# Channel attention on one core: TensorE waits for VectorE's partial sums, which are joined every third tile

## The chip, the cores and the metric

The kernel runs on 1 core of one Trainium2 chip. The metric is the device time of one execution in microseconds (us). Time before: median 527.9 us.

## The reference, cut to what matters

```python
# x: (1, 384, 384, 384) bfloat16, w1d: (1,) bfloat16
g = jnp.einsum("bhwc->bc", x) / (H * W)          # mean of every channel
s = jax.nn.sigmoid(g * w1d[0])                   # one factor for each of 384 channels
return x * s[:, None, None, :]
```

The input is 113.25 MB and so is the output. The factor depends on the mean over all of x, so taken literally x would be read twice. The kernel reads it once: it guesses the factors from the first 4 rows of the first tile, multiplies all tiles by the guess while it sums them, and at the end compares the true factors with the guess after rounding to bfloat16. Only if they differ does a second pass run. With the given inputs it doesn't.

## The kernel before

x is cut into 18 tiles of 64 rows a partition (6.29 MB). Four buffers hold them in turn. For each tile SyncE issues the load, TensorE adds up 48 rows with matmuls against a matrix of ones, VectorE adds up the other 16 rows and then multiplies the whole tile in place by the guess (the gate), and ScalarE's queue issues the store. The load of tile k + 4 waits until the store of tile k has landed.

```python
TILE, SLOTS, EARLY, LEAD, FORE, OWN = 64, 4, 4, 8, 32, 16
PAUSE = 9
...
def one(e, s):                                   # TensorE, one tile
    e.wait_ge(ready, 1).then_inc(ready, -1)      # the tile has landed
    for r, n in ((0, FORE), (FORE, TILE - OWN - FORE)):
        add_rows(e, 1, (slot(s) + r) * C, n, False, False).then_inc(plan.sems["tensor"], 1)
...
def sum_own(k):                                  # VectorE: 16 rows to one, then into the running sum
    plan.op("vector", lambda e: e.reduce_sum(to[:], view, axis=mybir.AxisListType.X), ...)
    if k:
        plan.op("vector", lambda e: e.tensor_tensor(own[:], own[:], part[:], ALU.add), ...)
...
def pause(r0):                                   # ScalarE: delays the fifth load
    to = at(base, PAUSE)
    plan.op("scalar", lambda e: e.activation(
        to, warm[:, 0:1].broadcast_to([P, PAUSE * C]), ACT_F.Sigmoid), ...)
```

At the end VectorE splits its running sum into three bfloat16 terms, TensorE adds these over the partitions, VectorE adds TensorE's three banks with six instructions (`add_banks`), ScalarE makes the true factors, and VectorE compares them and writes a flag. SyncE, ScalarE and VectorE read the flag to decide on the second pass.

## Time and profile before

| | before |
|---|---|
| median of the first 3 runs | 527.9 us (527.87 to 527.96) |
| span of the profiled run | 526.5 us |
| VectorE busy | 440.0 us, 78 instructions |
| DMA | 226.5 MB, 430 GB/s over the span |
| flag written | 521.4 us |
| last store issued, landed | 502.9, 526.4 us |

The busy shares, the DMA row and the chain of waits are shown in the prediction. Here is one steady tile on VectorE from the timeline of the kernel before (start, duration, engine, line, operation; in brackets the idle time and who ended it): the sum of 16 rows, the add, the gate.

```profile
170.19 10.56 DVE L338 TENSOR_REDUCE part<-arena 128x384 f32<-128x6144 bf16 x1 [4.94 <-DMA arena<-in_x_dram]
180.78 0.56 DVE L345 TENSOR_TENSOR own<-own,part 128x384 f32<-128x384 f32 x1
181.26 12.95 DVE L210 TENSOR_TENSOR arena<-arena,s_early 128x24576 bf16<-128x24576 bf16 x1
```

VectorE works 24 of 29 us and waits 4.94 us for the load. It has room, and the load is what it waits for.

### The profile page before, as it was taken

To read this page: it belongs to the slowest core of one execution; us is meant where nothing else is said; L and a number is where in the kernel's file an instruction comes from. 1 tells how busy PE (TensorE), PEld (TensorE's weight loads), DVE (VectorE), ACT (ScalarE), POOL (GpSimd) and SP (SyncE) were. 2 spreads that over 40 slices of the span, in tenths; PEclk is the share of its full clock that TensorE was granted. 3 is DMA by queue.
4 is the path that set the end of the run, shared out by engine and by line. 5 is a ranking of instruction groups with operands and counts; after the bars stand their busy time and mean duration, and the time that the engine had idled before them with its cause. 6 is when DMAs were issued, how large, how long until landed. Compare 5 with 4: busy or idle time off the path is not lost.

```text
span 526.5 us, 902 instructions
## 1 busy us (share of the span) xinstructions
PE 180.0 (34%) x648; PEld 0.2 (0%) x2; DVE 440.0 (84%) x78; ACT 5.8 (1%) x5; POOL 0.3 (0%) x6
## 2 busy tenths in 40 slices
PE   2255752043240707061422506070513315070701
PEld 0000000000000000000000000000000000000000
DVE  1869999999996978969696969789696969698795
ACT  1000020000000000000000000000000000000000
POOL 0000000000000000000000000000000000000000
PEclk9996967558585858567575858576675858585765
DMA  9999999999999999999999999999999999999998
GB/s 375 433 459 405 418 448 448 418 418 467 429 418 418 467 429 418 429 459 426 418 429 459 426 418 441 445 429 418 448 437 429 418 459 429 426 418 459 429 426 359
DMA packets 5620, 226.51 MB, mean 430 GB/s; under 512 B 626, under 2 KB 626, under 8 KB 754
## 3 DMA queue, kind: packets, MB, share of 16 engines
q10 hardware_dynamic: 3024, 122.29, 53.7%
q1 hardware_dynamic: 2594, 104.20, 46.0%
q14 instruction: 2, 0.02, 0.0%
HBM read 113.25 MB, written 113.25 MB: 430 GB/s over the span
## 4 chain that ended last, share of the span: by engine, by line
DMA 42%; another core or an unknown queue 27%; DVE 21%; issue 7%; SPq 0%; ACT 0%; DVEq 0%
DMA arena<-in_x_dram 24%; DMA out_dram<-arena 18%; DVE part L338 12%; DVE arena L210 7%; DVE own L345 1%; DVE total L326 0%; SPq L109 0%; DVE own L363 0%; DVE terms L356 0%; ACT arena L488 0%; DVE total L496 0%; DVE total L482 0%; DVE wrong L504 0%; DVE total L324 0%
## 5 line engine op out<-in xcount | busy, mean ns | idle before, releaser
L248 PE MATMUL acc<-arena,ones 128*128 128x512 bf16 x637 | 176.1, 441 | 312.2 <-PEq L292 310.8
L210 DVE TENSOR_TENSOR arena<-arena,s_early 128x24576 bf16<-128x24576 bf16 (+1 forms) x19 | 233.2, 12278 | 11.5 <-PE acc L248 6.5
L338 DVE TENSOR_REDUCE part<-arena 128x384 f32<-128x6144 bf16 x17 | 179.2, 10539 | 56.9 <-DMA arena<-in_x_dram 56.9
L338 DVE TENSOR_REDUCE own<-arena 128x384 f32<-128x6144 bf16 x1 | 10.4, 10435 | 0.6 <-DMA arena<-in_x_dram 0.6
L345 DVE TENSOR_TENSOR own<-own,part 128x384 f32<-128x384 f32 x17 | 9.5, 558 | 0.6
L425 DVE TENSOR_SCALAR w_scaled<-w_all 128x1 f32<-128x1 f32 x2 | 0.2, 152 | 8.0 <-PE w_all L416 8.0
L248 PE MATMUL acc_own<-terms,ones 128*128 128x384 bf16 x3 | 1.4, 479 | 15.3 <-DVE terms L356 15.3
L488 ACT ACTIVATE arena<-total,w_scaled 128x384 bf16<-128x384 f32 x1 | 0.6, 615 | 440.3 <-DVE total L482 440.3
L326 DVE TENSOR_TENSOR total<-total,acc 128x128 f32<-128x128 f32 (+2 forms) x10 | 3.9, 393 | 0.3
L399 ACT ACTIVATE arena<-warm 128x3456 bf16<-128x3456 f32 x1 | 3.1, 3082 | 61.9 <-DMA out_dram<-arena 61.9
L416 PE MATMUL w_all<-w_one,ones 1*128 1x1 bf16 x1 | 0.2, 158 | 9.3 <-DMA w_one<-in_w1d_dram 9.3
L248 PE MATMUL acc<-zeros,ones 128*128 128x512 bf16 x6 | 2.3, 507 | 0.0
L324 DVE COPY total<-acc 128x384 f32<-128x384 f32 x2 | 1.1, 554 | 1.2 <-PE acc L248 1.2
L410 ACT ACT_TABLE_LOAD x1 | 1.3, 1283 | 2.3 <-issue 2.3
L433 DVE MEMSET ones<- 128x128 bf16 x1 | 0.2, 165 | 1.3 <-PEq L611 1.3
L363 DVE TENSOR_TENSOR own<-own,terms 128x384 f32<-128x384 f32 x2 | 1.1, 559 | 0.1
L356 DVE CAST terms<-own 128x384 bf16<-128x384 f32 x3 | 1.1, 359 | 0.1
L496 DVE TENSOR_TENSOR total<-arena,s_early 128x384 f32<-128x384 uint16 x1 | 0.6, 558 | 0.7 <-ACT arena L488 0.7
L448 ACT ACTIVATE s_early<-total,w_scaled 128x384 bf16<-128x384 f32 x1 | 0.6, 614 | 9.8 <-DVE total L326 9.8
L482 DVE TENSOR_TENSOR total<-total,acc_own 128x384 f32<-128x384 f32 x1 | 0.6, 554 | 0.1
L246 PE MATMUL acc<-arena,ones 128*128 128x512 bf16 x1 | 0.6, 608 | 0.0
L504 DVE TENSOR_REDUCE wrong<-total 128x1 f32<-128x384 f32 x1 | 0.6, 553 | 0.0
(10 smaller groups left out, 1.2 us busy)
## 6 DMA issues: line engine op xcount, KB each, us to landing
out_dram<-arena ACTq DMA_DIRECT2D x18, 6144.0 KB, 49.9
arena<-in_x_dram SPq DMA_DIRECT2D x16, 6144.0 KB, 41.8
arena<-in_x_dram ACTq DMA_DIRECT2D x2, 3072.0 KB, 41.5
arena<-in_x_dram ACTq DMA_DIRECT2D x1, 2688.0 KB, 14.0
arena<-in_x_dram SPq DMA_DIRECT2D x1, 2688.0 KB, 21.4
arena<-in_x_dram SPq DMA_DIRECT2D x1, 768.0 KB, 7.8
w_one<-in_w1d_dram SPq DMA_DIRECT2D x1, 0.0 KB
```

The source lines that it names most:

```text
L210: return lambda e: e.tensor_tensor(to_v, v, s_b, ALU.mult)
L246: loaded.append(e.matmul(bank, weights, moving, start=start, stop=stop))
L248: return e.add_instruction(mybir.InstMatmult(name=nc.get_next_instruction_name(), engine=mybir.EngineType.PE, ins=[e.lower_ap(moving), e.l ...
L324: emit = lambda e, part=part, of=of: e.tensor_copy(part, of)
L326: emit = lambda e, part=part, of=of: e.tensor_tensor(part, part, of, ALU.add)
L338: lambda e: e.reduce_sum(to[:], view, axis=mybir.AxisListType.X),
L345: lambda e: e.tensor_tensor(own[:], own[:], part[:], ALU.add),
L356: lambda e, term=term: e.tensor_copy(term, own[:]),
L363: lambda e, term=term: e.tensor_tensor(own[:], own[:], term, ALU.subtract),
L399: lambda e: e.activation(to, warm[:, 0:1].broadcast_to([P, PAUSE * C]), ACT_F.Sigmoid),
L410: lambda e: e.activation(warm[:, 1:2], warm[:, 0:1], ACT_F.Sigmoid),
L448: lambda e: e.activation(s_early[:], total[:], ACT_F.Sigmoid, scale=w_scaled[:, 0:1]),
```

## The change

The intent is to take instructions off VectorE, 62 in place of 78 by the change's own words. The add after every sum goes; the sums stay as parts and are joined when four are there, which after the first four tiles is every third tile. VectorE's sum signals TensorE, whose last 4 rows wait for it, so that the gate needs to wait for TensorE alone. The six bank adds become one reduce, two small steps at the flag become one, and the second pass moves to GpSimd. The delay of the fifth load is remade, as its old scratch space now holds the parts.

```diff
-TILE, SLOTS, EARLY, LEAD, FORE, OWN = 64, 4, 4, 8, 32, 16
+TILE, SLOTS, EARLY, LEAD, FORE, OWN = 64, 4, 4, 8, 44, 16
+PARTS = 5
-PAUSE = 9
+PAUSE, PAUSES = 3, 3
...
         def one(e, s):
-            e.wait_ge(ready, 1).then_inc(ready, -1)
-            for r, n in ((0, FORE), (FORE, TILE - OWN - FORE)):
+            for of, r, n in ((ready, 0, FORE), (summed, FORE, TILE - OWN - FORE)):
+                e.wait_ge(of, 1).then_inc(of, -1)
                 add_rows(e, 1, (slot(s) + r) * C, n, False, False).then_inc(
...
-    def add_banks(group, copy):                 # six instructions
+    def total_of(group):
+        view = acc[group][:, :].rearrange("p (t c) -> p c t", c=C)
+        plan.op("vector", lambda e: e.reduce_sum(total[:], view, axis=mybir.AxisListType.X), ...)
...
     def sum_own(k):
+        plan.streams["vector"].append(
+            ("op", lambda e: e.reduce_sum(part(i), view, axis=mybir.AxisListType.X), summed, 1))
+        plan._record(all_summed[k], reads, writes)
+        kept.append(i)
-        if k:
-            plan.op("vector", lambda e: e.tensor_tensor(own[:], own[:], part[:], ALU.add), ...)
+    def join_parts(to=None): ...                # one reduce over the parts that are kept
...
     def pause(r0):
-        to = at(base, PAUSE)
-        plan.op("scalar", lambda e: e.activation(to, warm[:, 0:1].broadcast_to([P, PAUSE * C]), ...
+        to, of = terms[:, : PAUSE * C], warm[:, 0:1].broadcast_to([P, PAUSE * C])
+        for i in range(PAUSES):
+            plan.op("scalar", lambda e: e.activation(to, of, ACT_F.Sigmoid), ...
...
+    def put_tile(k):
+        sum_own(k)
+        put(slot(k), TILE, row0(k), parts=None if k else (FORE, TILE - FORE))
+        if len(kept) == PARTS - 1:
+            join_parts()
```

More of the change, by code (lines that the diff above doesn't have):

```diff
@@ L183, in bass_standalone__channel_attn_eca__vision_kernel @@
     warm = nc.alloc_sbuf_tensor("warm", [P, 2], F32)
-    wrong = nc.alloc_sbuf_tensor("wrong", [P, 1], F32)
     redo = nc.alloc_sbuf_tensor("redo", [P, 1], I32)
@@ L188, in bass_standalone__channel_attn_eca__vision_kernel @@
     own = nc.alloc_sbuf_tensor("own", [P, C], F32)
-    part = nc.alloc_sbuf_tensor("part", [P, C], F32)
     terms = nc.alloc_sbuf_tensor("terms", [P, 3 * C], BF16)
@@ L192, in bass_standalone__channel_attn_eca__vision_kernel @@
     arena = nc.alloc_sbuf_tensor("arena", [P, n_arena * C], BF16)
-    acc = [
-        [nc.alloc_psum_tensor(f"acc{g}_{i}", [P, WIDE], F32) for i in range(3)]
-        for g in range(2)
-    ]
+    acc = [nc.alloc_psum_tensor(f"acc{g}", [P, 3 * WIDE], F32) for g in range(2)]
     w_all = nc.alloc_psum_tensor("w_all", [P, WIDE], F32)
-    acc_own = nc.alloc_psum_tensor("acc_own", [P, WIDE], F32)
     def at(r0, n):
@@ L213, in bass_standalone__channel_attn_eca__vision_kernel @@
     base = SLOTS * TILE
-    assert n_rows % TILE == 0 and base + PAUSE <= n_arena
+    assert n_rows % TILE == 0 and base + 2 * PARTS <= n_arena
     assert EARLY % 4 == FORE % 4 == (TILE - OWN) % 4 == 0 and EARLY <= LEAD <= FORE
@@ L217, in bass_standalone__channel_attn_eca__vision_kernel @@
     ready = nc.alloc_semaphore("ready")
+    summed = nc.alloc_semaphore("summed")
     def slot(k):
@@ L265, in add_rows @@
                 e,
-                acc[group][i % 3][:, :],
+                acc[group][:, i % 3 * WIDE : (i % 3 + 1) * WIDE],
                 ones[:],
@@ L286, in nothing @@
         none = zeros[:, 0:1].broadcast_to([P, WIDE])
-        return mm(e, acc[1][bank][:, :], ones[:], none, start, not start)
+        to = acc[1][:, bank * WIDE : (bank + 1) * WIDE]
+        return mm(e, to, ones[:], none, start, not start)
     def sum_all():
         def one(e, s):
-            e.wait_ge(ready, 1).then_inc(ready, -1)
-            for r, n in ((0, FORE), (FORE, TILE - OWN - FORE)):
+            for of, r, n in ((ready, 0, FORE), (summed, FORE, TILE - OWN - FORE)):
+                e.wait_ge(of, 1).then_inc(of, -1)
                 add_rows(e, 1, (slot(s) + r) * C, n, False, False).then_inc(
@@ L309, in emit, with part, part_rows @@
                             one(e, s)
-            for i in range(3):
-                done = nothing(e, i, False)
-            done.then_inc(plan.sems["tensor"], 1)
+            for i in (1, 2):
+                nothing(e, i, False)
         plan.streams["tensor"].append(("block", emit, None))
-    def add_banks(group, copy):
-        for m, lo, hi in ((0, 0, C), (0, C, WIDE), (1, 0, 256), (1, 256, WIDE),
-                          (2, 0, P), (2, P, WIDE)):
-            c = (128 * m + lo) % C
-            part = total[:, c : c + hi - lo]
-            of = acc[group][m][:, lo:hi]
-            if copy and (m, lo) == (0, 0):
-                emit = lambda e, part=part, of=of: e.tensor_copy(part, of)
-            else:
-                emit = lambda e, part=part, of=of: e.tensor_tensor(
-                    part, part, of, ALU.add
-                )
-            plan.op("vector", emit, reads=[f"acc{group}", "total"], writes=["total"])
+    def total_of(group):
+        view = acc[group][:, :].rearrange("p (t c) -> p c t", c=C)
+        plan.op(
+            "vector",
+            lambda e: e.reduce_sum(total[:], view, axis=mybir.AxisListType.X),
+            reads=[f"acc{group}"],
+            writes=["total"],
+        )
+    def part(i, n=1):
+        return at(base + 2 * i, 2 * n).bitcast(F32)
+    def part_rows(i, n=1):
+        return rows(base + 2 * i, 2 * n)
+    kept, free = [], list(range(PARTS - 1))
+    all_summed = []
     def sum_own(k):
@@ L334, in sum_own, with join_parts @@
         view = at(r0, OWN).rearrange("p (t c) -> p c t", t=OWN)
-        to = part if k else own
+        i = free.pop(0)
+        reads, writes = rows(r0, OWN), part_rows(i)
+        for token in plan._needs(reads, writes):
+            plan._wait("vector", token)
+        plan.streams["vector"].append(
+            (
+                "op",
+                lambda e: e.reduce_sum(part(i), view, axis=mybir.AxisListType.X),
+                summed,
+                1,
+            )
+        )
+        plan._record(all_summed[k], reads, writes)
+        kept.append(i)
+    def join_parts(to=None):
+        lo, n = min(kept), len(kept)
+        assert sorted(kept) == list(range(lo, lo + n))
+        i = 0 if lo else PARTS - 1
+        view = part(lo, n).rearrange("p (t c) -> p c t", c=C)
+        out = part(i) if to is None else to[:]
         plan.op(
             "vector",
-            lambda e: e.reduce_sum(to[:], view, axis=mybir.AxisListType.X),
-            reads=rows(r0, OWN),
-            writes=["part" if k else "own"],
-        )
-        if k:
-            plan.op(
-                "vector",
-                lambda e: e.tensor_tensor(own[:], own[:], part[:], ALU.add),
-                reads=["own", "part"],
-                writes=["own"],
-            )
+            lambda e: e.reduce_sum(out, view, axis=mybir.AxisListType.X),
+            reads=part_rows(lo, n),
+            writes=["own"] if to is not None else part_rows(i),
+        )
+        kept[:] = [i]
+        free[:] = range(1, PARTS - 1) if i == 0 else range(PARTS - 2, 0, -1)
     def join_own():
@@ L372, in join_own @@
                 "tensor",
-                lambda e, i=i, term=term: mm(
-                    e, acc_own[:, :C], ones[:], term, i == 0, i == 2
-                ),
+                lambda e, term=term: mm(e, acc[1][:, :C], ones[:], term, False, False),
                 reads=["ones", f"term{i}"],
-                writes=["acc_own"],
+                writes=["acc1"],
             )
+        plan.op(
+            "tensor", lambda e: nothing(e, 0, False), reads=["zeros"], writes=["acc1"]
+        )
     def put(place, n, r0, to=None, parts=None):
@@ L394, in pause @@
     def pause(r0):
-        to = at(base, PAUSE)
-        plan.op(
-            "scalar",
-            lambda e: e.activation(
-                to, warm[:, 0:1].broadcast_to([P, PAUSE * C]), ACT_F.Sigmoid
-            ),
-            reads=["warm"],
-            writes=rows(r0, 1) + ["pause"],
-        )
+        to, of = terms[:, : PAUSE * C], warm[:, 0:1].broadcast_to([P, PAUSE * C])
+        for i in range(PAUSES):
+            plan.op(
+                "scalar",
+                lambda e: e.activation(to, of, ACT_F.Sigmoid),
+                reads=["warm"],
+                writes=["pause", "term0", "term1", "term2"] + ([] if i else rows(r0, 1)),
+            )
     def weight():
@@ L432, in bass_standalone__channel_attn_eca__vision_kernel @@
     plan.op("gpsimd", lambda e: e.memset(warm[:, 0:1], 0.0), writes=["warm"])
-    plan.op("vector", lambda e: e.memset(ones[:], 1.0), writes=["ones"])
+    plan.op("gpsimd", lambda e: e.memset(ones[:], 1.0), writes=["ones"])
     plan.op("gpsimd", lambda e: e.memset(zeros[:], 0.0), writes=["zeros"])
@@ L444, in bass_standalone__channel_attn_eca__vision_kernel @@
     sum_early()
-    add_banks(0, copy=True)
+    total_of(0)
     plan.op(
@@ L460, in bass_standalone__channel_attn_eca__vision_kernel @@
             for i in range(2) if k == SLOTS else () if k < SLOTS + 2 else (k - SLOTS,):
-                sum_own(i)
-                put(slot(i), TILE, row0(i), parts=None if i else (FORE, TILE - FORE))
+                put_tile(i)
             if k == SLOTS:
@@ L468, in bass_standalone__channel_attn_eca__vision_kernel @@
         plan.signals("tensor", rows(slot(k) + FORE, TILE - OWN - FORE), ["acc1"])
-    plan.signals("tensor", [], ["acc1"])
+        all_summed.append((plan.sems["tensor"], plan.count["tensor"]))
     for k in range(n_tiles - SLOTS, last):
-        sum_own(k)
-        put(slot(k), TILE, row0(k))
+        put_tile(k)
     put(slot(last), TILE, row0(last), slot(n_tiles))
     sum_own(last)
+    join_parts(own)
     join_own()
-    add_banks(1, copy=True)
-    plan.op(
-        "vector",
-        lambda e: e.tensor_tensor(total[:], total[:], acc_own[:, :C], ALU.add),
-        reads=["acc_own", "total"],
-        writes=["total"],
-    )
+    total_of(1)
     plan.op(
@@ L503, in bass_standalone__channel_attn_eca__vision_kernel @@
         "vector",
-        lambda e: e.reduce_max(wrong[:], total[:], axis=mybir.AxisListType.X),
+        lambda e: e.reduce_max(redo[:], total[:], axis=mybir.AxisListType.X),
         reads=["total"],
-        writes=["wrong"],
-    )
-    plan.op(
-        "vector",
-        lambda e: e.tensor_copy(redo[:], wrong[:]),
-        reads=["wrong"],
         writes=["redo"],
@@ L523, in bass_standalone__channel_attn_eca__vision_kernel @@
         again.op(
-            "vector",
+            "gpsimd",
             gate(place, place, n, s_true),
@@ L580, in _ @@
             plan.emit("vector", e)
-            second_pass("vector", e)
         @block.scalar
@@ L594, in _ @@
             plan.emit("gpsimd", e)
+            second_pass("gpsimd", e)
     for token in plan.final:
```

## The prediction

> **What bounds the kernel now.** I read the page first (busy shares, then the slices), because one look tells whether an engine or the DMA is full.
>
> ```profile
> span 526.5 us, 902 instructions
> ...
> PE 180.0 (34%) x648; PEld 0.2 (0%) x2; DVE 440.0 (84%) x78; ACT 5.8 (1%) x5; POOL 0.3 (0%) x6
> ...
> DMA  9999999999999999999999999999999999999998
> ...
> HBM read 113.25 MB, written 113.25 MB: 430 GB/s over the span
> ```
>
> VectorE looks busy at 84%, but only the DMA row has a 9 in nearly every slice. 226.5 MB must move whatever the engines do (113.25 read, 113.25 written), and the change alters no byte of it. Next I asked for the stretches between fixed times, to see whether the rate differs by stage:
>
> ```profile
> 0.00:45.00 45.00, 13.99 (x44) 0.20 (x2) 26.89 (x13) 2.10 (x3) 0.33 (x6) 0.93 0.99 418
> ...
> 195.00:224.00 29.00, 9.51 (x35) 0.00 (x0) 23.99 (x3) 0.00 (x0) 0.00 (x0) 0.68 1.00 434
> ...
> 502.90:524.20 21.30, 1.44 (x3) 0.00 (x0) 17.30 (x17) 0.61 (x1) 0.00 (x0) 0.50 1.01 436
> 524.20:526.50 2.30, 0.00 (x0) 0.00 (x0) 0.00 (x0) 0.00 (x0) 0.00 (x0) 0.50 0.02 4
> ```
>
> The last three columns are TensorE's clock, DMA share and GB/s. The rate is 432 to 436 in the steady stage and in the tail; the 418 of the head contains about 1.6 us before the first bytes. Busy share is 1.00 or so everywhere. So the DMA is full from about 1.6 to 524.2 us, and what is left is edges: 1.6 us ahead and 2.3 us of completion after. Third, the chain of waits, for a turn of the ring that a buffer makes (there are 4 buffers of 64 rows):
>
> ```profile
> 331.76 42.07 DMA arena<-in_x_dram
> 373.83 0.02 issue
> 373.86 10.58 DVE part L338
> 384.44 0.02 issue
> 384.46 0.56 DVE own L345
> 385.02 12.88 DVE arena L210
> 397.90 0.02 issue
> 397.92 49.83 DMA out_dram<-arena
> ...
> 489.92 12.96 DVE arena L210
> 502.88 10.34 DVE part L338
> ```
>
> A load, VectorE's sum of 16 rows, the add into the running sum, the gate (the multiply that makes the output) and the store: 42.07 + 10.58 + 0.56 + 12.88 + 49.83 and small gaps make 116.0 us, four tiles of 29.0. This looks like a ring limited by latency. But a tile of 6.29 MB takes only 14.5 us at 434 GB/s; that load and store last 42 and 50 us shows that they wait behind each other. Their length is an outcome of the full DMA, not a cost of its own. The waits say the same: VectorE stands idle about 5 us a tile for a load.
>
> ```profile
> L338 DVE TENSOR_REDUCE part<-arena 128x384 f32<-128x6144 bf16 x17 | 179.2, 10539 | 56.9 <-DMA arena<-in_x_dram 56.9
> L345 DVE TENSOR_TENSOR own<-own,part 128x384 f32<-128x384 f32 x17 | 9.5, 558 | 0.6
> ```
>
> [...]the reduce here reads rows 768 B apart and takes 10539 / 6144 = 1.72 ns an element, against 558 / 384 = 1.45 ns, fixed cost included, for the dense add. [...]the granted clock here is 0.50 between tiles and 1.00 from the middle of a tile's matmuls[...].
>
> **The change, part by part.** (1) 17 adds of 558 ns go: 9.5 us. In their place come 5 joins of 4 parts and, at the end, one of 3. At 1.72 ns an element (estimate from the sum's row) a join of 4 x 384 elements is 2.6 us and of 3 x 384 is 2.0 us: 5 x 2.6 + 2.0 = 15.0 us added. The five come after a store is issued, where VectorE has 5 us to spare.
> (2) The last 4 rows of a tile (3 matmuls) wait for VectorE's sum, and the gate waits for them. Sum to gate was 0.5 us (a sum starts at 170.19 and its gate at 181.26, and the sum is 10.56). Now it is a semaphore (0.05, as between cast and matmul in the tail), one matmul of 379 to 630 ns and two more at about 0.22, and a semaphore back: 0.9 to 1.1 us. A tile's store is issued some 0.5 us later. VectorE's needs per tile: 10.57 + 1.0 + 12.95 + 2.6/3 = 25.4 us of 29.0, so it still waits for loads.
> (3) First part of the first tile 44 rows, not 32: the gate began at 31.08, after 24 matmuls; 9 more at about 0.22 put it at 33.0, and the first store from 44.1 to about 46.1. The loads still in flight fill this: the fourth tile's load landed at about 72, so the DMA has work.
> (4) The pause of 3.08 us becomes three activations. With 0.61 us for 384 elements and 3.08 for 3456, one of 1152 takes about 1.2 us: 3.7 in all. The fifth load goes out 0.6 us later while the second store runs alone at the full rate: free.
> (5) The six adds of the banks (1.1 / 2 + 3.9 / 2 = 2.5 us each time, with gaps 2.7) become one reduce of 4 x 384 elements from PSUM, [...]2.6 at the sum's rate. The early one is hidden.
> (6) The tail: last sum ends at 513.2, the flag was written at 521.4, so 8.2 us. Now: join 2.0, the three casts and two subtractions 2.3 as before, the last matmul and the empty one 0.9, bank reduce 2.6, sigmoid 0.65, compare 0.6, maximum straight into the flag 0.6: 9.7 us, ending at 522.9. The last store was issued at 502.9 and took 23.5 to land: 526.4. So the longer tail is still hidden, with about 3.5 us for reading the flag.
> (7) The second pass moves from VectorE to GpSimd; it isn't executed, only the flag is read there. By my count VectorE issues 54 counted instructions, not 62; I can't place the other 8. Its busy time goes 440.0 - 9.5 - 5.0 - 0.6 - 0.3 + 15.0 + 2 x 2.6 = about 445 us: fewer instructions, not less time.
> The sum on the path that sets the end: nothing, as bytes and rate stay: 527.9 us, plus perhaps 0.1 for the later gates.
>
> **The rivals.** (A) The ring is the bound, and each 0.56 us gone from it counts: 116.0 - 2.2 us per four tiles would give about 518 us, 1.9% less. For it: the chain runs through the add 17 times. Against it: [...]the new trip to TensorE takes back what the add gave. (B) The tail shows. If the sum's 10.54 us hold a fixed cost per output instead of one per element[...], then join and bank reduce are 5.3 and 5.7 us, the tail 16.2 us, the flag at 529.4 and the time 531 to 533: 0.6 to 1.0% slower. One row cannot tell the two. (C) VectorE becomes the bound: with trip 1.6 (half clock) and join 5.7 it needs 10.57 + 1.6 + 12.95 + 5.7/3 = 27.0 us a tile, still below 29.0. Stores have room too: the one issued at about 426.9 is 20.8 us ahead of the landing of its forerunner at 447.75. To starve the DMA, all of this must go: not likely, about 540 if so.
>
> **Range and chances.** Main case 0.8: 527.3 to 528.4. Case B 0.12: up to 533, more probably partly hidden, 529 to 531. Case A in part 0.05: down to 526. So 528.0, range 526.9 to 529.5. Over 2% faster (below 517.3)[...]: 0.01. Over 2% slower (above 538.5) needs case C or an unseen stall: 0.03.
>
> **What would show it.** Right: the DMA row stays at 9 with 430 GB/s over the span; the 29.0 us between tiles stays; the gate starts 0.9 to 1.1 us after its sum; VectorE's busy time stays within 10 us of 440 with its idle time for loads at about 3 us a tile; the joins at 2.0 to 2.6 us. Wrong: a slice of the DMA below 9 before the last one (C), a tile period under 28.8 us (A), or a flag written after 525 us with the span as much longer (B).

Rival A's sum came to 524.6 us, so that at most 3 us could be had, and rested on a ceiling of the DMA's rate that was not shown. The traced rates give nearly the same, as an estimate: at the 434 to 436 GB/s of the views above 226.51 MB take 519.5 to 521.9 us, with the edges of 3.9 us 523.4 to 525.8, so 0.7 to 3.1 us of the 526.5.

Rival B's 5.3 and 5.7 us, and with them its tail of 16.2 and time of 531 to 533 us, and C's join of 5.7, came from 10.8 ns an output, worked out with a cost per element that was not shown. The bank adds in the profile before give one: 286, 420 and 554 ns for 128, 256 and 384 elements, 1.05 ns for each further element. With it the estimate is 10540 / 384 - 16 x 1.05 = 10.6 ns an output, and again 5.3 and 5.7 us. The low end of the bank reduce, 1.6 us, rested on the same cost: 1536 x 1.05 ns is 1.6. That a wait of about 1 us would not drop TensorE's clock was concluded from a rule; the profile after shows one such wait: over 1.05 us without work (209.25 to 210.30 us) the granted clock stayed at 1.00.

## The result, and the profile after

| | before | after |
|---|---|---|
| median, first comparison (6 runs each) | 527.89 us (527.80 to 528.22) | 528.92 us (528.01 to 530.22) |
| median, all runs | 527.97 us (37 runs) | 528.97 us (11 runs) |
| middle half of all runs | 527.87 to 528.20 | 528.48 to 529.29 |

The ratio of the first comparison is 1.0019 with a 95% interval of 1.0005 to 1.0033. Ratios are the mean time of one kernel's fast runs over that of the other's of the same rounds, so not quite the ratio of the medians quoted. So the change is the same within 2%, and a shade slower: about 1 us in the medians, with a scatter of 2 us where the kernel before mostly stays within half a us (one of its 37 runs took 532.2).

The page of the changed kernel, busy shares, the DMA row and the bytes:

```profile
span 527.8 us, 900 instructions
...
PE 186.2 (35%) x661; PEld 0.2 (0%) x2; DVE 443.8 (84%) x54; ACT 6.2 (1%) x7; POOL 0.5 (0%) x7
...
DMA  9999999999999999999999999999999999999997
...
HBM read 113.25 MB, written 113.25 MB: 429 GB/s over the span
```

VectorE (DVE) has 24 instructions fewer and 3.8 us more work. The DMA row is as full as before; only the very last slice has gone from 8 to 7. The groups of instructions of the changed kernel tell why VectorE gained nothing (line, engine, operation, shapes, count; then busy us, mean ns of one, idle us before them and what ended it):

```profile
L352 DVE TENSOR_REDUCE arena<-arena 128x384 f32<-128x6144 bf16 x18 | 189.2, 10509 | 36.8 <-DMA arena<-in_x_dram 36.7
L369 DVE TENSOR_REDUCE arena<-arena 128x384 f32<-128x1536 f32 x5 | 13.8, 2752 | 0.0
...
L322 DVE TENSOR_REDUCE total<-acc 128x384 f32<-128x1536 f32 x2 | 3.5, 1758 | 2.2 <-PE acc L245 2.2
```

Five joins of 2752 ns cost more than the 17 adds that they replace (9.5 us). The idle time for loads fell from 56.9 to 36.7 us. Where the rest of it went stands in the list of who waited for whom, again of the changed kernel (us in total, times, longest):

```profile
DVE arena L206 <- PE acc L245: 25.3, 17, 7.4
```

The gate (L206) now waits for TensorE. In a steady tile of the changed kernel's timeline it looks like this:

```profile
199.63 10.56 DVE L352 TENSOR_REDUCE arena<-arena 128x384 f32<-128x6144 bf16 x1 [0.64 <-DMA arena<-in_x_dram]
211.15 12.96 DVE L206 TENSOR_TENSOR arena<-arena,s_early 128x24576 bf16<-128x24576 bf16 x1 [0.96 <-PE acc L245]
```

From the start of a sum to its gate it was 11.07 us before and is 11.52 now. Yet the period of the tiles is unchanged: the sums that start at 287.46 and 462.18 us are six tiles apart, 29.1 us each, and those of the kernel before (286.40 and 460.85) also 29.1. What VectorE loses to TensorE it waits less for loads.

So where is the 1 us? The end. These are the last stretches of the two kernels in steps of 1 us (start:end, then busy times; the last three columns are TensorE's clock, the DMA share and GB/s). Before:

```profile
523.00:524.00 1.00, 0.00 (x0) 0.00 (x0) 0.00 (x0) 0.00 (x0) 0.00 (x0) 0.50 1.13 492
524.00:525.00 1.00, 0.00 (x0) 0.00 (x0) 0.00 (x0) 0.00 (x0) 0.00 (x0) 0.50 0.15 57
525.00:526.00 1.00, 0.00 (x0) 0.00 (x0) 0.00 (x0) 0.00 (x0) 0.00 (x0) 0.50 0.00 0
```

After:

```profile
524.00:525.00 1.00, 0.00 (x0) 0.00 (x0) 0.53 (x1) 0.00 (x0) 0.00 (x0) 0.50 0.12 49
525.00:526.00 1.00, 0.00 (x0) 0.00 (x0) 0.00 (x0) 0.00 (x0) 0.00 (x0) 0.50 0.12 49
526.00:527.00 1.00, 0.00 (x0) 0.00 (x0) 0.00 (x0) 0.00 (x0) 0.00 (x0) 0.50 0.00 0
527.00:527.80 0.80, 0.00 (x0) 0.00 (x0) 0.00 (x0) 0.00 (x0) 0.00 (x0) 0.50 0.03 10
```

These views count a packet in the stretch in which it starts, so what they show after 524 us is packets that start late, and not all that is still moving. By the records of the packets, the last big one (49152 B) of the kernel before starts at 524.09 us and ends at 525.92. In the changed kernel the two stretches with 49 GB/s hold one such packet each: they start at 524.67 and 525.34 and end at 526.49 and 527.25. They overlap, so two engines are late. The trace records 16 increments of the last store's semaphore, at different times. I take them for one from each of the core's 16 DMA engines: in the changed kernel the last two come at 526.84 and 527.76 us, 0.35 and 0.52 us after the two late packets have ended. So one can look at the last store engine by engine. The next lines are worked out from these records (us from the span's start):

```
kernel    first    median   third last   second last   last     last minus first
before    524.96   525.22   525.73       525.98        526.41   1.46
after     524.82   525.14   525.94       526.84        527.76   2.94
```

Most engines end at the same time in both. In the changed kernel the last engine is 1.35 us later, as much as the spans differ by: 526.5 and 527.8. This is what the experiments had to explain, besides testing what the prediction rests on. I call the last column the spread.

The records of the packets give the floor. The bulk of the bytes moves in packets of 49152 B that take 1.815 us each (median), 27.1 GB/s an engine or 433 GB/s for 16. 226.51 MB are 288.0 such packets an engine, 522.7 us, and the first ones start at 1.0 to 1.5 us: an estimate of 523.7 to 524.2 us. In both kernels 13 of the 16 engines end their last big packet between 524.4 and 525.3 us, up to 1 us after it. The record doesn't number the engines, but packets can be strung together by their times; in both kernels no row so made has a gap of over 0.25 us. A late engine is therefore not an idle one: it has had longer packets, nearly all of them in the queue of SyncE's loads (10.6 of 11.7 us of excess before, 12.3 of 12.8 after). Summed over all engines, the time of these packets above 1.815 us is nearly the same in both kernels (11.7 us before, 12.8 after); what differs is how unevenly it falls on the 16.

### The profile page after: what moved, and what is told of

Its sections match the earlier page's. It is cut to its first block, busy times and chain, and to the rows that moved or that the text cites. A ratio compares the mean times of both kernels' runs of the same rounds, so it can differ in the third digit from the quotient of the medians.

```text
span 527.8 us, 900 instructions
## 1 busy us (share of the span) xinstructions
PE 186.2 (35%) x661; PEld 0.2 (0%) x2; DVE 443.8 (84%) x54; ACT 6.2 (1%) x7; POOL 0.5 (0%) x7
## 2 busy tenths in 40 slices
DMA packets 5620, 226.51 MB, mean 429 GB/s; under 512 B 626, under 2 KB 626, under 8 KB 754
## 5 line engine op out<-in xcount | busy, mean ns | idle before, releaser
L245 PE MATMUL acc<-arena,ones 128*128 128x512 bf16 x650 | 181.7, 444 | 323.4 <-PEq L295 323.4
L206 DVE TENSOR_TENSOR arena<-arena,s_early 128x24576 bf16<-128x24576 bf16 (+2 forms) x19 | 233.3, 12285 | 29.9 <-PE acc L245 25.3
L352 DVE TENSOR_REDUCE arena<-arena 128x384 f32<-128x6144 bf16 x18 | 189.2, 10509 | 36.8 <-DMA arena<-in_x_dram 36.7
L369 DVE TENSOR_REDUCE arena<-arena 128x384 f32<-128x1536 f32 x5 | 13.8, 2752 | 0.0
L322 DVE TENSOR_REDUCE total<-acc 128x384 f32<-128x1536 f32 x2 | 3.5, 1758 | 2.2 <-PE acc L245 2.2
L427 ACT ACTIVATE terms<-warm 128x1152 bf16<-128x1152 f32 x3 | 3.5, 1162 | 62.8 <-DMA out_dram<-arena 62.7
L369 DVE TENSOR_REDUCE own<-arena 128x384 f32<-128x1152 f32 x1 | 1.5, 1471 | 1.6 <-PE acc L245 1.6
L245 PE MATMUL acc<-terms,ones 128*128 128x384 bf16 x3 | 1.4, 477 | 2.1 <-DVE terms L382 2.1
L243 PE MATMUL acc<-arena,ones 128*128 128x512 bf16 x1 | 0.6, 606 | 0.0
```

The costliest lines, as they stand in the source:

```text
L206: return lambda e: e.tensor_tensor(to_v, v, s_b, ALU.mult)
L243: loaded.append(e.matmul(bank, weights, moving, start=start, stop=stop))
L245: return e.add_instruction(mybir.InstMatmult(name=nc.get_next_instruction_name(), engine=mybir.EngineType.PE, ins=[e.lower_ap(moving), e.l ...
L322: lambda e: e.reduce_sum(total[:], view, axis=mybir.AxisListType.X),
L352: lambda e: e.reduce_sum(part(i), view, axis=mybir.AxisListType.X),
L369: lambda e: e.reduce_sum(out, view, axis=mybir.AxisListType.X),
```

## The experiments

Twelve runs were made, in three jobs of four, each job on another chip. Those of one job share the runs of the kernel before.

**Once more as it is.** No edit.

> The changed kernel as it is, once more, against the kernel before in the same rounds. Question: is the +1.0 us (528.92 against 527.89) and the wide scatter (2.2 us against 0.4 us over 6 runs) of the change or of the chip that ran it? My theory (skew): all 16 DMA engines work without a gap in both kernels, most of them end at the same time (the median of the last store's 16 landings is 525.2 us before and 525.1 after), and the change only lets one engine fall behind the others (last landing 526.4 before, 527.8 after). It expects 528.0 to 530.2 again with scatter over 1 us. Rival (chip noise): 527.7 to 528.2 with scatter below 0.5 us.

Measured: 528.97 us (527.87 to 529.72, 5 runs), ratio 1.0010, interval 0.9997 to 1.0024; spread of the last store 3.25 us. The kernel before in this job: 527.98 (527.83 to 528.85). The scatter belongs to the changed kernel on this chip as well, though the interval of the ratio now reaches 1.

**No trip to TensorE.**

```diff
-            for of, r, n in ((ready, 0, FORE), (summed, FORE, TILE - OWN - FORE)):
-                e.wait_ge(of, 1).then_inc(of, -1)
+            e.wait_ge(ready, 1).then_inc(ready, -1)
+            for r, n in ((0, FORE), (FORE, TILE - OWN - FORE)):
```

and in `sum_own` an ordinary VectorE operation in place of the one that signals `summed`.

> The changed kernel with one part undone: TensorE's last 4 rows no longer wait for VectorE's sum, so the gate need not wait for TensorE (VectorE keeps its parts and the joins every third tile). If the trip to TensorE costs time on the path, as a ring bound by latency would have it (0.96 to 1.59 us of VectorE's idle time per tile, 17 times, spread over 4 buffers: 4 to 6 us), the time falls to about 523 to 525 us. My theory (DMA full): VectorE's idle time moves from TensorE to loads, the time stays within 1 us of the changed kernel's, 527.8 to 529.5; at most the skew of the DMA engines changes.

Measured: 528.65 us (527.98 to 531.09, 6 runs), ratio 1.0005, interval 0.9991 to 1.0018; the spread of the profiled run, which was the slowest, is 4.82 us. The list of who waited for whom in this run:

```profile
DVE arena L348 <- DMA arena<-in_x_dram: 53.4, 12, 5.9
DVE arena L206 <- PE acc L245: 7.5, 2, 7.3
```

The waits for TensorE fell from 25.3 to 7.5 us and those for loads rose from 36.7 to 53.4. Of 17.8 us won, 16.7 went straight into waiting for the DMA, and the time stayed. So the trip is not on the path that sets the end, and it isn't the cause of the spread either.

**32 rows ahead of the wait.**

```diff
-TILE, SLOTS, EARLY, LEAD, FORE, OWN = 64, 4, 4, 8, 44, 16
+TILE, SLOTS, EARLY, LEAD, FORE, OWN = 64, 4, 4, 8, 32, 16
```

> The changed kernel with 32 rows ahead of the wait in place of 44, so 16 rows (12 matmuls) follow VectorE's sum. The gate then waits some 2.7 to 4.6 us for TensorE instead of 1.0 to 1.6. DMA full: the time stays within 1 us, 527.8 to 529.5, though VectorE needs about 2 us more a tile. Ring bound by latency: another 2 to 3 us in each of 18 tiles over 4 buffers, 8 to 12 us longer, 537 to 541.

Measured: 546.64 us (544.58 to 548.60, 5 runs), ratio 1.036. Both expectations missed; it is far outside of mine. The page and the list of waits of this run:

```profile
span 543.1 us, 887 instructions
...
DMA  9999999999999999999999999999999999995893
```

```profile
DVE arena L206 <- PE acc L245: 78.4, 17, 5.4
...
DVE arena L352 <- DMA arena<-in_x_dram: 3.5, 2, 2.2
```

The gates wait 78.4 us in all, 4.6 us each. VectorE's idle time for loads is used up, 3.5 us of 36.7. A steady tile then needs 10.4 + 4.6 + 13.0 us and a third of a join (0.9), 28.9 us, which is the DMA's own pace of 29.1. VectorE has become the bound: it starts the last store at 517.8 us where the changed kernel does at 504.2, and the DMA runs dry ahead of it (the 5 and the 8 in its row; the packets show 15 of the 16 engines without work for some 9 us, until the store before the last starts at 505.8, and the last of them from 503.5). My error was to hold VectorE's need against the period alone: an engine that needs about as much as the period can't catch up what it is late by in the first tiles. The 12 matmuls after the wait, at 4.3 us, also took the upper end of what I had allowed.

This run gives one more number. Its last store landed at 535.5 us, but the span ends at 543.1; the end of the chain of waits is

```profile
540.27 0.55 DVE redo L529
```

so from the flag at 540.8 to the end are 2.3 us, which I put down to reading it and ending the program.

**A shorter delay of the fifth load.**

```diff
-        to, of = terms[:, : PAUSE * C], warm[:, 0:1].broadcast_to([P, PAUSE * C])
+        to, of = terms[:, :988], warm[:, 0:1].broadcast_to([P, 988])
```

> The changed kernel with its three activations that delay the fifth load cut from 1152 to 988 elements, so that they take about 3.1 us as in the kernel before, in place of 3.5. If the offset between load and store queue set by that delay decides the skew of the DMA engines, the extra 1 us and the scatter go (527.7 to 528.3, scatter below 0.6). If it does not, 528.0 to 530.2 stays.

Measured: 527.92 us (527.85 to 528.74, 5 runs), ratio 0.9999, interval 0.9985 to 1.0013; spread 1.43 us. That looked like the cause found: all of the change but the longer delay, and the 1 us is gone. It had to be turned around and repeated.

> The changed kernel with the short delay (3.14 us) again, to see whether the first result (527.92, four of five runs within 527.85 to 527.97) holds: 527.8 to 528.2 in most runs, ratio 1.000, last landings spread by about 1.4 us. If the first was luck: 528.3 to 529.5 with a scatter over 1 us.

Measured on repetition: 528.43 us (527.95 to 531.39, 7 runs), ratio 0.9997, interval 0.9971 to 1.0022; the profiled run is the one of 531.39, with a spread of 5.07 us. The same program now scattered. The first result was in part luck.

**The change's delay alone, in the kernel before.** Its `pause` was replaced by the one of the change, 3.55 us in place of 3.08.

> The kernel before with one part of the change alone: the delay ahead of the fifth load becomes three activations of 1152 elements (3.55 us) in place of one of 3456 (3.08 us), so that this load goes out some 0.4 us later. The run with the delay cut back (pause308) brought the changed kernel to 527.92. If the delay alone makes the skew of the DMA engines, this one shows 528.2 to 529.5 with a scatter over 1 us, and the last store's 16 landings are spread by 2.5 us or more (1.46 before). If the delay needs the rest of the change to hurt, it stays at 527.8 to 528.2 and a spread near 1.5 us.

Measured: 528.59 us (528.04 to 529.43, 5 runs), ratio 1.0009, interval 0.9996 to 1.0022; spread 2.30 us. Repeated:

> The kernel before with the change's delay (3.55 us) again: 528.59 the first time with an interval that just held 1. If the delay is the cause: 528.2 to 529.5, scatter over 1 us. If the first was luck: 527.8 to 528.2.

Measured: 528.13 us (527.70 to 528.98, 6 runs), ratio 0.9997, interval 0.9971 to 1.0023; spread 1.82 us. Between the two expectations; inconclusive by itself.

**Other delays.** In the changed kernel, `PAUSES` and the width of the activation were set for about 4.95, 5.37 and 2.7 us; the traces show 5.00, 5.39 and 2.73. The edit of the first:

```diff
-PAUSE, PAUSES = 3, 3
+PAUSE, PAUSES = 3, 5
...
-        to, of = terms[:, : PAUSE * C], warm[:, 0:1].broadcast_to([P, PAUSE * C])
+        to, of = terms[:, :921], warm[:, 0:1].broadcast_to([P, 921])
```

The second has 1020 in place of 921. The third has 824 and leaves `PAUSES` at 3.

> The changed kernel with a delay of about 4.95 us (five activations of 921 elements), which is 3.14 us plus 1.815 us, the time of one 48 KB packet on a DMA engine. If what counts is where the fifth load falls in the cycle of packets (phase), this is as good as 3.14 us: 527.8 to 528.3, spread of the last landings near 1.4 us. If the skew grows with the delay, or any delay other than the old one is bad: 528.5 to 530.5, spread of 2.5 us or more.

Measured: 528.86 us (527.95 to 531.11, 6 runs), ratio 1.0023, interval 1.0007 to 1.0039; spread of the profiled run, a quick one of 528.41, 1.81 us. For the time, my idea of a phase that repeats with every packet is refuted: the interval leaves out 1. For the state in which the engines leave the delay it is not, as the table of spreads below shows.

> The changed kernel with a delay of about 5.37 us (five activations of 1020 elements), which is the change's 3.55 us plus one packet of 1.815 us. Phase: as bad as the changed kernel, 528.3 to 530, spread of 2.5 us or more. Growing with the delay: worse than that. A late load alone that costs nothing: 527.8 to 528.2.

Measured: 529.11 us (528.19 to 531.05, 6 runs), ratio 1.0020, interval 1.0003 to 1.0036; spread 3.92 us.

> The changed kernel with a delay of about 2.7 us (three activations of 824 elements). If the old delay is a hit that was searched for (a packet of 1.815 us on each engine, and a load that goes out 0.4 us later or earlier finds the engines in another order), 2.7 may miss it: 528.2 to 530 with scatter. If short delays are good in general: 527.8 to 528.2 and two engines one packet apart from the rest from the fifth load on (spread of its landings over 2 us).

Measured: 528.94 us (527.81 to 529.99, 6 runs), ratio 1.0013, interval 0.9987 to 1.0040; the profiled run is the quickest, 527.81, with a spread of 1.12 us. A shorter delay is not better as such. Of all delays tried, only the one near 3.1 us has a median at 528.0, and not in every job.

**Half of two stores left out.** Wrong: the output lacks 64 rows a partition.

```diff
-        put(slot(k), TILE, row0(k), parts=None if k else (FORE, TILE - FORE))
+        put(slot(k), TILE, row0(k), parts=None if k else (FORE, TILE - FORE), rows_out=32 if k in (8, 10) else None)
```

> Wrong result on purpose: the changed kernel with the short delay (pause308) writes only half of the rows of two tiles, so 6.29 MB or 2.8% less moves, while every engine does the same work. DMA full all the way: 6.29 MB at 433 GB/s is 14.5 us less, 513 to 514 us. VectorE or its ring as the bound: no less than 524 us. In between if VectorE, which idles 34 us for loads in pause308, comes to be the bound part of the way.

Measured: 513.41 us (513.29 to 513.58, 4 runs), ratio 0.9721. The page:

```profile
HBM read 113.25 MB, written 106.95 MB: 430 GB/s over the span
```

2.8% fewer bytes took 2.8% off the time, to 0.1 us what the rate foretells from pause308's 527.92 (from the 528.43 of its repetition it would be 0.5 us), while VectorE and TensorE did all of their work. A shorter store also shortens the ring, so this run alone doesn't tell the two apart; but no_trip gave the ring 17 us back and won no time. The two together show that the DMA bounds the kernel.

**A longer tail.** Three more reduces over 4 parts after the last join, with the short delay.

```diff
     join_parts(own)
+    for _ in range(3):
+        extra = part(0, 4).rearrange("p (t c) -> p c t", c=C)
+        plan.op("vector", lambda e: e.reduce_sum(total[:], extra, axis=mybir.AxisListType.X), ...)
```

> The changed kernel with the short delay and three more joins of 4 parts (2.75 us each, results thrown away) on VectorE in the tail. In pause308 the flag stood at 523.3 us and in fore32 the end came 2.26 us after the flag, so the tail reaches 525.6 of 526.4: 0.9 us to spare. With 8.3 us more the flag stands at 531.6, the end at 533.9 and the time, 1.5 us over the span, at 535.4. If the tail were hidden beyond that, 527.9; if it were on the path already, 536.2.

Measured: 535.11 us (534.82 to 538.29, 4 runs), ratio 1.0146. The chain of waits of this run ends with

```profile
530.71 0.55 DVE redo L537
```

and its span is 533.5: again 2.3 us from the flag to the end. The changed kernel's flag stands at 524.5, so its tail would end at 526.8, 1 us ahead of the last landing at 527.8. The kernel before had 2.7 us to spare (521.4 + 2.3 against 526.4). The tail has become longer and is still hidden, but only just: more than a microsecond would show.

**What all profiled runs say together of the spread.** Fourteen profiled runs are at hand. I leave out fore32, where the DMA runs dry, and set for the others the spread of the second store, landing at 96 to 100 us and the first after the delay, beside that of the last store (worked out from the 16 increments of each, us):

```
run             second store   last store
pause270        1.94           1.12
half_stores     2.66           1.28
pause308        2.30           1.43
before          2.37           1.46
tail_long       2.32           1.67
pause495        2.66           1.81
before_p350_b   0.59           1.82
before_p350     0.44           2.30
after           0.55           2.94
after_again     0.50           3.25
pause536        0.71           3.92
no_trip         0.61           4.82
pause308_b      0.73           5.07
```

The two groups, the six upper rows and the seven lower ones, don't overlap, though 1.81 and 1.82 lie close. Counted from the packets between 104 and 115 us, in before, pause308, tail_long and pause495 two engines move a store packet while the other 14 move a load packet, and the other way round; in pause270 they split 9 to 7. In all seven of the lower group at least 15 engines move loads at the same time and then stores at the same time: they have come out of the delay in step. The packets alone don't part the groups, though: half_stores, of the upper one, has 15 engines together too. Later one or two of them fall behind; in the changed kernel the spread grows from 0.55 to 2.94 us little by little. In fore32, which is left out, all engines are in step at 100 us but one already lags, and the spread of a store grows from 3.9 us (the second) to 10.4 (landing at 465 us) before the DMA runs dry. Whether an execution comes out in step or apart is settled by the time the second store lands, soon after the fifth load has gone out. It differs between executions of one program (a spread of 2.30 us in pause308, 0.73 in pause308_b), so the delay can at most change the odds.

That it does change them, the table says more clearly than the times. All five runs of the table with the change's 3.55 us are in the lower group (the two of the kernel before among them), and four of the five with 3.08 or 3.14 us in the upper. Six of these ten are in the lower group; if the delay had no part in it, all five with 3.55 us would be among the six in only 5 of 210 ways. The longer delays follow the idea of a phase, too: 5.00 us, one packet after 3.14, is in the upper group, and 5.39, one packet after 3.55, in the lower. I sorted the runs after seeing them, and there is one run of each longer delay, so this is a strong hint and not a test.

## Why the prediction was right, and where it was not

The measured 528.92 us lies in the range of 526.9 to 529.5, and "within 2%" is right. That the range holds it is in part luck: its part above 528.4 was there for case B, a tail that shows, and the microsecond came from elsewhere. Point by point:

**The bound.** Right, and shown by half_stores and no_trip: bytes over rate is the time, about 433 GB/s in the full stages. The steps (1), (2), (4) and (5) moved VectorE's work by some us and the period of 29.1 us stayed. One reading was wrong: the row 524.20:526.50 with a share of 0.02 was taken for 2.3 us of completion after a DMA that is done. That view counts packets where they start; big packets were moving until 525.92 us, and the span ends at 526.5, just after the last increment at 526.41.

**The sizes.** The join of 4 parts: 2.6 foretold, 2.75 measured; of 3 parts: 2.0, measured 1.47. The trip: 0.9 to 1.1 foretold, 0.96 measured in steady tiles; but 1.59 in four early tiles, where VectorE runs late and TensorE has idled for 6.4 to 16.3 us before the last 3 matmuls, which then run at a granted clock of 0.50. The bank reduce: between 1.6 and 2.6, measured 1.76. By layout one element of these reduces cost 1.72 ns (bfloat16, 768 B apart), 1.79 ns (4 float32 parts, 2752 ns for 1536), 1.28 ns (3 float32 parts, 1471 ns for 1152) and 1.14 ns (PSUM, 1758 ns for 1536), fixed costs included; why 3 and 4 parts differ was not shown. VectorE's busy time: 445, measured 443.8, and 54 instructions. The first gate: 33.0, measured 32.08. The delay: 3.7, measured 3.55. The tail from the last sum to the flag: 9.7, measured 10.0 (514.5 to 524.5), as a join of 3 parts was quicker but first waits 1.6 us for TensorE, which I had not listed.

**The rivals.** (A), the ring as a bound, is refuted by no_trip: 17 us given back to VectorE went into waiting for loads. (B), a tail that shows, did not come about: it had put the last join and the bank reduce at 5.3 and 5.7 us (my estimate, see beside the prediction), and they took 1.47 and 1.76; tail_long shows that it was nearer than the "about 3.5 us for reading the flag" made it seem, since the reading and the end of the program alone take 2.3. (C), VectorE as the bound, did not come about, but my working of its margin was wrong: I put 27.0 us a tile below 29.0 and asked for a 20 us delay to starve the DMA. In fore32 it needed 28.9 us a tile and lost 18 us. The room that counts is VectorE's idle time for loads over the whole run, 56.9 us before and 36.7 after.

**The step that failed** is the sum: "The sum on the path that sets the end: nothing, as bytes and rate stay: 527.9 us, plus perhaps 0.1 for the later gates." The bytes and the rate of most engines did stay. But the last store was over only with its last increment (527.76 us of 527.8 after), and the prediction treated the DMA as one server. The last engine's lag after the first, 1.46 us before and 2.94 after, accounts for the added time in the two profiled runs (1.35 us between their last landings). The median of 528.92 is outside of the main case (527.3 to 528.4), to which I gave 0.8.

**What stays open.** That the added time is the late engine is shown by the landings. That executions with a small spread after the delay end late is a regularity of 13 profiled runs, not a proven cause. Why an engine's load packets grow longer in these is not known; that all engines read at one time and then write at one time, and that a straggler reads while the others write, is only a guess. That the longer delay raises the odds fits the pooled runs: 7 of 12 runs of pause308 and its repetition end by 528.1 us, 26 of 37 of the kernel before, 4 of 11 with the change's delay in the kernel before, 2 of 11 of the changed kernel. But the intervals of pause308, before_p350 and their repetitions all hold 1, so by the times it is not settled, nor is it how much of the 1 us the rest of the change adds. No version with a right result ran faster than the kernel before by a margin that its interval confirms.

## What to carry to other kernels

Here the DMA was full from end to end, and a shorter chain on VectorE turned into waiting time for it (16.7 of 17.8 us in no_trip). Test this in another kernel by taking away bytes, and by taking away work, and see which of the two moves the time; here 2.8% fewer bytes took 2.8% off it. Count an engine's slack as its idle time over the whole run, and spend it knowingly: a wait of 4.6 us in a tile, which one number in this kernel brings, made VectorE the bound and cost 18 us. Differences of a few tenths of a per cent need the times of all 16 DMA engines (here the last landed 1.12 to 5.07 us after the first for the last store) and repeated jobs before a part of a change is blamed; a first run that fits the theory (pause308) may not be repeated.
